# Two Q units between the fold blocks, residual copies two tiles ahead, sums by quarter: one change in four parts to a fused attention and mixer block

## The chip, the cores and the metric

The kernel runs on one core of one Trainium2 chip. The metric is the device time of one execution in microseconds (us). A profiled execution stands beside the timed runs; its span is the time from the first to the last instruction of the core.

Engines are named as in the profile: PE is the matrix engine (PEld its weight loads), DVE the vector engine, ACT the scalar engine, POOL the general engine, SP the engine that issues most of the DMAs. SPq is SP's queue.

## The reference

`x` is 2048 x 1024 (S x D) in bf16. The block is two residual parts:

```
h  = x + o(LN(x)) @ wo          # linear attention, 32 heads of 32
     q, k, v = split(LN(x) @ wqkv);  phi(t) = where(t > 0, t + 1, exp(t)) + 1e-6
     kv = phi(k)^T v per head;  z = sum over rows of phi(k)
     o  = (phi(q) kv) / (phi(q) . z + 1e-6)
h2 = h + mixer(LN(LN(h)))       # LN of LN: the mixer normalizes its own input again
     u  = gelu(hn^T @ w1 + b1)          # w1: 2048 x 3584, over the rows of x
     y  = (u @ w2 + b2)^T               # w2: 3584 x 2048
```

## The kernel before, in words

**Products in blocks of seven.** All large products are done as two-by-two block products with seven multiplications instead of eight: sums of blocks of the one operand (`asum`, `asums`, `x_sums`) and of the other (`combine`, `inner_moving`, `w_sums`) are made on DVE, and PE adds seven products into PSUM tiles. In the mixer, two of the seven (later more) are again split by seven (`Inner`, `Inner2`). A product's method `mm` (L355) walks over the `nk` blocks of the contracted dimension, one 128 x 128 x 512 matmul each.

**Order.** Most instructions are kept in program order on their engine by `pin` or by the wrappers `hv` (DVE), `ht` (PE), `hs` (ACT), `hd` (SP DMAs), so the order in which the Python code issues them is the order on each engine. A tile of a pool waits for the last reader of the buffer that it gets.

**Stage 1, to about 163 us in the profile: K, V, Q.** Rows of x are normalized and transposed (`ln_finish`). From row pair 2 on, K and V of two row tiles are a step each (`KRun`, `VRun`), and Q of a quarter of the rows comes in steps `QRun` with pairs 5 and 7 and after them. `run_step` (L1239) interleaves a step with the rest of the previous one. Q of the first quarter is done in eight plain units of eight matmuls: `q_unit` (L1419) and, later, `q_held` (L1645). Each unit's phi is one Exp and one Relu on ACT and two operations on DVE. `q_fill` takes the next of the eight. Three are issued around the first V step, one each after step `p7` of K and V of pair 6 (`fill_at`, L1463), one in the last `run_step`. Two are left for the fold stretch.

**Fold stretch, 163 to 177 us.** `kv` and `wo` are multiplied into one weight per head: `fold(n)` (L1629), n = 0 to 3, is 16 matmuls of 32 x 32 x 512 into four PSUM tiles; ACT and DVE copy these to `wf` (fp16): block 1 on DVE, for the second half of the columns (n = 1, 3) block 3 too, the others on ACT. Folds 0 and 2 give columns 0 to 511, folds 1 and 3 the rest. `den_mm` makes the denominators of a quarter of rows, `den_inv` their reciprocals, `den_spread` sends them through DRAM to all partitions, and `scale_q` (DVE, 128 x 2048) multiplies phi(q) by them. `q_held(units[0])` uses one of two PSUM banks of the pool of the denominators (`den_tile`), as do two tiles of `fold(2, 2)`. All others come from `acc_tile` (L83), a ring of six banks in two pools of four and two.

**Output projection, 169 to 229 us: loop over 16 row tiles** (L1810), in the order of quarters 2, 3, 1, 0 (`SPREAD`, `order`). Tile i is two halves of eight matmuls (`out_mm`), evacuated by `out_evac`. For the first nine tiles (`SEEDED` = 9) a DMA from POOL adds x to the evacuated tile (L1715); means and squares come from ACT's accumulators or DVE. From tile 9 on the residual is put into the PSUM bank ahead of the matmuls: `seed(i)` (L1673) is two ACT copies of the loaded row tile (`load_xr`), and DVE takes the statistics straight from PSUM. `h_var` and `store_h` issue the tile's store on SP; `h_scale` is Ln and Exp on ACT; `normalize_h` (DVE) writes the even row tiles into `hE`, the odd into `hO`; as soon as a pair is there, `combine_h` (L1758) makes its four sums, each 128 x 512: T3 = O.hi - E.hi, E.hi = E.hi - E.lo, T2 = O.hi - E.hi, T4 = O.lo - T2. W1 is loaded in column groups of 512 in four parts (`load_w1`, L146): group 0 in the fold stretch, group 1 at tiles 5, 7, 9 and 11 (`w1_at`). `first_sums` makes the first weight sums of the mixer in between.

In this loop a seed of tile i+1 stands first in iteration i from tile 10 on; seeds of 9 and 10 come in iterations 7 and 8, behind `out_evac(i)`.

**Mixer, 229 us to the end.** PSUM pools psy, psx, psw, psz of two banks each are opened (L1861). `sums5` makes the four inner sums of E.hi (128 x 1024 each), then `run_first` (L759) does product 1 (E.lo), product 2 (O.lo), then inner product 5 mixed with product 6 (T2), then 7 (T3) and 3; product 4 (T4) comes with the next pair of column groups. Mixer 1 contracts over eight row blocks, in the order 0 to 7: block k holds row tiles 2k (in `hE`) and 2k+1 (in `hO`). The last quarter of the projection, quarter 0, is blocks 0 and 1; quarter 1 is blocks 2 and 3.

Of the kernel before, what the change touches and what calls it, by code (L numbers as in the profile page):

```python
# [24 lines left out]
SEEDED = 9  # L25
# [8 lines left out]
def kernel(  # L34
# [144 lines left out]
    def combine(e, o, t2, t3, t4, v=nc.vector):  # L179
        lo, hi = slice(0, CW), slice(CW, 2 * CW)  # L180
        sub = ALU.subtract
        v.tensor_tensor(t3, o[:, hi], e[:, hi], sub)
        v.tensor_tensor(e[:, hi], e[:, hi], e[:, lo], sub)
        v.tensor_tensor(t2, o[:, hi], e[:, hi], sub)
        if t4 is not None:
            v.tensor_tensor(t4, o[:, lo], t2, sub)

# [144 lines left out]
    class Product7:  # L332
        def __init__(self, p, w, nk, mov):
# [21 lines left out]
        def mm(self, m, ps, start, ks=None, cols=slice(0, CW)):  # L355
            lhs, mv = self.lhs[m], self.mov[m]
            for k in range(self.nk) if ks is None else ks:
                pe.matmul(
                    ps[:, cols],
                    lhsT=lhs[:, k, :],  # L360
                    rhs=mv(k)[:, cols],
                    start=(start and k == 0),
                    stop=(k == self.nk - 1),
                    skip_group_check=True,
                )
# [73 lines left out]
    class Mixer1(Product7):  # L439
        def __init__(self, p):  # L440
# [428 lines left out]
    with ExitStack() as actx:  # L869
# [33 lines left out]
        with ExitStack() as a1:  # L903
# [559 lines left out]
            fill_at = {("K", 6, 0), ("V", 6, 0)}  # L1463
# [161 lines left out]
        with ExitStack() as a3:  # L1625
# [125 lines left out]
            def normalize_h(i, combined=True):  # L1751
# [3 lines left out]
                if combined and i ^ 1 in normal:  # L1755
                    combine_h(i)

            def combine_h(i):  # L1758
                q = order[i] // 2
                combine(hE[:, q, :], hO[:, q, :], hT2[:, q, :], hT3[:, q, :], hT4[:, q, :], hv)  # L1760
# [18 lines left out]
            fold(2, 2)  # L1779
            scale_q(2, 1)  # L1780
            load_w1(0, 1, pin, 4)
            q_held(*units[1])
            fold(1)
            load_w1(0, 2, pin, 4)
            xctx.close()
# [23 lines left out]
            w1_at = {5: (1, 0), 7: (1, 1), 9: (1, 2), 11: (1, 3)}  # L1809
            for i in range(1, NS):  # L1810
                if i > SEEDED:
                    seed(i + 1)
# [8 lines left out]
                if i == NS - 1:  # L1821
                    h_scale(i - 1)
                    normalize_h(i - 2, False)
# [3 lines left out]
                if i - 3 in BY_ACT:  # L1827
                    normalize_h(i - 3)
                if i > 1:
# [3 lines left out]
                if SEEDED - 2 <= i < SEEDED:  # L1833
                    seed(i + 2)
# [15 lines left out]
                if SEEDED + 2 <= i < NS - 1:  # L1850
                    normalize_h(i - 2)
            h_scale(NS - 1)
            normalize_h(NS - 1, False)
            combine_h(NS - 3)
            combine_h(NS - 1)
# [4 lines left out]
    NT = 2  # L1860
# [229 lines left out]
```

## Time and profile before

| what | value |
|---|---|
| timed runs | 553.98, 555.28, 552.6 us; median 553.98 |
| profiled execution, its own time | 553.12 us |
| its span | 551.3 us |
| granted PE clock | 1.000 |
| fold stretch, first held Q unit to the den matmuls of tile 1 | 162.75 to 177.39 us |
| output projection, den matmuls of tile 3 to the first mixer product | 184.95 to 229.30 us |

A row of the timeline is: start, length in us, engine, line, operation, output<-input, partitions x elements and type, count; in brackets the idle time of the engine before it and what ended it. Matmul lengths include the drain of the pipeline, so the distance between starts says how fast PE goes. A row of the waits list is: the engine and its tile, the releaser, total us, times, longest. A row of the windows view is: stretch, length, busy time of PE, PEld, DVE, ACT, POOL (with counts), granted clock, share of the DMA engines, GB/s.

### The profile page before, as it was taken

To read this page: it belongs to the slowest core of one execution; us is meant where nothing else is said; L and a number is where in the kernel's file an instruction comes from. 1 tells how busy PE (TensorE), PEld (TensorE's weight loads), DVE (VectorE), ACT (ScalarE), POOL (GpSimd) and SP (SyncE) were. 2 spreads that over 40 slices of the span, in tenths; PEclk is the share of its full clock that TensorE was granted. 3 is DMA by queue.
4 is the path that set the end of the run, shared out by engine and by line. 5 is a ranking of instruction groups with operands and counts; after the bars stand their busy time and mean duration, and the time that the engine had idled before them with its cause. 6 is when DMAs were issued, how large, how long until landed. Compare 5 with 4: busy or idle time off the path is not lost.

```text
span 551.3 us, 10262 instructions
## 1 busy us (share of the span) xinstructions
PE 542.7 (98%) x3978; PEld 331.8 (60%) x3978; DVE 462.6 (84%) x904; ACT 292.3 (53%) x630; POOL 42.3 (8%) x54
## 2 busy tenths in 40 slices
PE   8999999999999998999999999999999999999997
PEld 3444446646763443456666767667455667877865
DVE  7798898866776698989989789897989899979877
ACT  5747777777687778545546465464320312413321
POOL 1000000000002350000000000000002102103111
PEclk9999999999999999999999999999999999999999
DMA  9933531200537999203140440413497659399344
GB/s 300 311 78 76 78 82 35 40 0 3 153 110 212 210 278 355 98 2 112 42 153 9 145 137 19 153 33 102 125 315 210 187 123 243 80 289 236 68 136 76
DMA packets 84513, 74.61 MB, mean 135 GB/s; under 512 B 16098, under 2 KB 77040, under 8 KB 84464
## 3 DMA queue, kind: packets, MB, share of 16 engines
q1 hardware_dynamic: 77344, 67.46, 41.6%
q0 software_dynamic: 6688, 6.04, 7.7%
q8 instruction: 31, 0.51, 0.4%
q10 hardware_dynamic: 432, 0.44, 0.2%
q14 instruction: 18, 0.15, 0.1%
HBM read 59.12 MB, written 11.67 MB: 128 GB/s over the span
## 4 chain that ended last, share of the span: by engine, by line
PE 89%; issue 2%; DMA 2%; ACT 2%; DVE 2%; POOL 1%; SPq 0%; DVEq 0%; POOLq 0%; ACTq 0%
PE psI L245 28%; PE psC L245 17%; PE psB L245 8%; PE acc_t L245 4%; PE psC L1071 4%; PE psB L1071 4%; PE psA L1071 4%; PE psA L245 3%; PE acc_t L987 3%; PE psE L1071 2%; PE psA L1205 2%; PE psC L1205 2%; PE psB L1205 2%; PE acc_t L1422 2%; POOL h_bf L1715 1%
## 5 line engine op out<-in xcount | busy, mean ns | idle before, releaser
L245 PEld LDWEIGHTS <-is 128*128 128x128 f16 x820 | 80.1, 98 | 31.5 <-DVE hi L245 0.4
L245 PEld LDWEIGHTS <-wq 128*128 128x128 bf16 (+1 forms) x610 | 59.6, 98 | 38.6 <-issue 1.0
L245 PEld LDWEIGHTS <-sa 128*128 128x128 f16 x571 | 55.8, 98 | 20.7
L245 PE MATMUL acc_t<-wo_sb,pqT 128*128 128x512 f16 x256 | 56.3, 379 | 3.0 <-ACT acc_t L245 2.2
L513 POOL DMA_DIRECT2D out_dram<-wq x28 | 24.4, 949 | 310.9 <-DMA wq<-in_B_w_dram 191.0
L245 PEld LDWEIGHTS <-pqT 128*128 128x128 bf16 x256 | 24.8, 98 | 33.9 <-issue 3.6
L245 PE MATMUL psC<-gs,wq 128*128 128x512 f16 x168 | 40.8, 379 | 0.0
L1071 PEld LDWEIGHTS <-xs 128*128 128x128 f16 x208 | 20.0, 98 | 22.2
L245 PE MATMUL psC<-hT,sa 128*128 128x512 f16 x112 | 31.2, 379 | 0.0
L1715 POOL DMA_DIRECT2D h_bf<-in_A_x_dram x18 | 15.9, 995 | 186.3 <-PE acc_t L245 171.1
L245 PE MATMUL psI<-hi,is 128*128 128x256 f16 x200 | 30.0, 273 | 0.0
L245 PE MATMUL psB<-hT,sa 128*128 128x512 f16 x112 | 29.7, 379 | 0.0
L245 DVE TENSOR_TENSOR t<-psI,t 128x256 f32<-128x256 f32 (+1 forms) x45 | 20.8, 475 | 9.4 <-PE psI L245 7.9
L245 PE MATMUL psC<-hT,wq 128*128 128x512 f16 x112 | 28.4, 379 | 0.0
L245 PE MATMUL psI<-gi,is 128*128 128x256 f16 x210 | 27.8, 273 | 0.0
L1071 PE MATMUL psA<-wkv,xnT 128*128 128x512 bf16 x104 | 26.7, 379 | 0.0
L1071 PEld LDWEIGHTS <-xnT 128*128 128x128 bf16 x156 | 15.3, 98 | 17.8 <-issue 0.2
L198 DVE TENSOR_SCALAR e_sb<-e_sb 128x512 bf16<-128x512 bf16 x64 | 18.2, 284 | 7.6 <-ACT e_sb L193 7.4
L245 ACT COPY psI<-psI 128x256 f32<-128x256 f32 x50 | 18.0, 360 | 11.7 <-PE psI L245 9.8
L245 DVE TENSOR_TENSOR sa<-wq 128x2048 f16<-128x2048 bf16 (+1 forms) x17 | 20.0, 1178 | 2.8 <-DMA wq<-in_B_w_dram 2.8
L987 PE MATMUL acc_t<-wkv,xnT 128*128 128x512 bf16 x96 | 21.7, 379 | 0.1
L956 DVE BATCH_NORM_STATS2 st<-x_sb 128x6 f32<-128x512 bf16 x32 | 20.6, 682 | 0.9 <-DMA x_sb<-in_A_x_dram 0.9
(266 smaller groups left out, 1145.4 us busy)
## 6 DMA issues: line engine op xcount, KB each, us to landing
wq<-in_B_w_dram SPq DMA_DIRECT2D x10, 1024.0 KB, 7.1
wq<-in_B_w_dram SPq DMA_DIRECT2D x20, 448.0 KB, 6.6
gs<-parked SPq DMA_DIRECT2D x9, 896.0 KB, 4.8
shared_sb<-rd_dram SPq DMA_DIRECT2D x32, 128.0 KB, 3.9
wq<-in_B_w_dram SPq DMA_DIRECT2D x8, 512.0 KB, 7.8
out_dram<-h_bf SPq DMA_DIRECT2D x16, 256.0 KB, 5.9
x_sb<-in_A_x_dram SPq DMA_DIRECT2D x14, 256.0 KB, 4.1
w2o<-in_B_w_dram SPq DMA_DIRECT2D x4, 896.0 KB, 10.2
```

The source lines that it names most:

```text
L198: pin(nc.vector.tensor_scalar(e_sb[:], e_sb[:], 1.0, PHI_EPS, ALU.min, ALU.add))
L245: return (lambda *a, **kw: pin(op(*a, **kw))) if self.always or getattr(Held, self.key) else op
L513: nc.gpsimd.dma_start(to, ot[:, a:b], accum_op=ALU.add)
L956: return nc.vector.bn_stats(st[:, c, :], x_sb[:, c * CW:(c + 1) * CW])
L987: mm = nc.tensor.matmul(pp[:, 0:CW], lhsT=xnT[:, kt, i * P:(i + 1) * P], rhs=wkv[:, kt, c * CW:(c + 1) * CW], start=(kt == 0), stop=(kt == ...
L1071: pin(nc.tensor.matmul(ps[:], lhsT=lhs[:, k, :], rhs=rhs[:, k, :], start=(start and k == 0), stop=(k == hk2 - 1), skip_group_check=True,))
L1205: pin(nc.tensor.matmul(out[:, j], lhsT=rhs[:, k, 2 * self.half + j, :], rhs=lhs[:, k], start=(start and j == 0 and k == 0), stop=(k == hk2 ...
L1422: nc.tensor.matmul(qp[:, 0:SW], lhsT=wq_sb[:, kt, j * P:(j + 1) * P], rhs=xnT[:, kt, u * SW:(u + 1) * SW], start=(kt == 0), stop=(kt == ND ...
L1715: nc.gpsimd.dma_start(h_bfs[i][:, cols], x[rows(i), cols], accum_op=ALU.add)
```

## The change

Four things are changed.

1. `fill_at` is empty: the K and V steps of pair 6 have no Q unit. Four units are left for the fold stretch: one before fold 0 (den bank), one after fold 0 (ring bank), one after fold 2 and one after fold 1 (den banks). `fold(2)` takes all its tiles from the ring.
2. `seed(i + 2)` for i = 7 to 13 stands ahead of `out_evac(i)`. Group 1 of W1 is loaded at tiles 9 to 12.
3. `combine` is gone. `sums_h(u, which)` makes the sums of a whole quarter (four row tiles) in operations of 128 x 2 x 512: of quarter 2 at tiles 7 and 8, of quarter 3 at tiles 11 and 12, of quarters 1 and 0 without T4 after the last statistics, with the normalization of tile 15 between them. T4 of those two quarters is one operation of 128 x 4 x 512 after `sums5`.
4. `Mixer1.first = NSP // 4` = 2: its products walk the row blocks in the order 2, 3, 4, 5, 6, 7, 0, 1. The four PSUM pools of the mixer are opened in the opposite order.

```diff
@@ -176,15 +176,6 @@
             for ks in spans:
                 load_w2(p, second, ks=ks)
 
-    def combine(e, o, t2, t3, t4, v=nc.vector):
-        lo, hi = slice(0, CW), slice(CW, 2 * CW)
-        sub = ALU.subtract
-        v.tensor_tensor(t3, o[:, hi], e[:, hi], sub)
-        v.tensor_tensor(e[:, hi], e[:, hi], e[:, lo], sub)
-        v.tensor_tensor(t2, o[:, hi], e[:, hi], sub)
-        if t4 is not None:
-            v.tensor_tensor(t4, o[:, lo], t2, sub)
-
     def phi_parts(dst, src, n, pool, view=lambda t: t, lean=False):
         e_sb = pool.tile([P, n], BF16, tag="phi_e", name="e_sb")
         r_sb = None if lean else pool.tile([P, n], BF16, tag="phi_r", name="r_sb")
@@ -330,6 +321,8 @@
             self.sink(0, 1, self.b)
 
     class Product7:
+        first = 0
+
         def __init__(self, p, w, nk, mov):
             self.p, self.nk, self.mov = p, nk, mov
             (self.a11, self.a21), (self.a12, self.a22) = [[v[:, :, h * P:(h + 1) * P] for h in range(2)] for v in w]
@@ -355,10 +348,11 @@
         def mm(self, m, ps, start, ks=None, cols=slice(0, CW)):
             lhs, mv = self.lhs[m], self.mov[m]
             for k in range(self.nk) if ks is None else ks:
+                at = (k + self.first) % self.nk
                 pe.matmul(
                     ps[:, cols],
-                    lhsT=lhs[:, k, :],
-                    rhs=mv(k)[:, cols],
+                    lhsT=lhs[:, at, :],
+                    rhs=mv(at)[:, cols],
                     start=(start and k == 0),
                     stop=(k == self.nk - 1),
                     skip_group_check=True,
@@ -437,6 +431,8 @@
                 self.after(self.done, late)
 
     class Mixer1(Product7):
+        first = NSP // 4
+
         def __init__(self, p):
             c = (p % 2) * 2 * P
             w = w1_tiles[p // 2][:, :, c:c + 2 * P].rearrange("p (k two) f -> p k two f", two=2)
@@ -1460,7 +1456,7 @@
             q_sums = {2: slice(0, 1), 3: slice(1, 2), 4: slice(2, 3), 5: slice(3, 4)}
             late_parts, late_home = sums_home(2)
             moved_at = {("K", 7, 0): ((3, 0), (3, 1)), ("V", 7, 0): ((4, 0), (4, 1))}
-            fill_at = {("K", 6, 0), ("V", 6, 0)}
+            fill_at = set()
             late_sums = {("K", 6): ((2, slice(0, 2)),), ("K", 7): ((2, slice(2, 4)), (3, slice(0, 1))), ("V", 7): ((3, slice(1, 4)),)}
             for q in range(2, NVP):
                 runs = [KRun(q), VRun(q)]
@@ -1748,16 +1744,25 @@
                 hs.activation(lnv[:], mv_all[:, i, 1:2], ACT.Ln, bias=eps2[:], scale=(1.0 + LN_EPS) * share_of)
                 hs.activation(sc_all[:, i:i + 1], lnv[:], ACT.Exp, scale=-0.5)
 
-            def normalize_h(i, combined=True):
+            def normalize_h(i):
                 dst = hE if i % 2 == 0 else hO
                 hv.tensor_scalar(dst[:, order[i] // 2, :], h_bfs.pop(i)[:], mv_all[:, i, 0:1], sc_all[:, i:i + 1], ALU.subtract, ALU.mult)
                 normal.add(i)
-                if combined and i ^ 1 in normal:
-                    combine_h(i)
-
-            def combine_h(i):
-                q = order[i] // 2
-                combine(hE[:, q, :], hO[:, q, :], hT2[:, q, :], hT3[:, q, :], hT4[:, q, :], hv)
+
+            lo, hi = slice(0, CW), slice(CW, D)
+
+            def sums_h(u, which=("t3", "t1", "t2", "t4")):
+                assert normal.issuperset(range(NSC * SPREAD.index(u), NSC * SPREAD.index(u) + NSC))
+                ks = slice(NSC // 2 * u, NSC // 2 * (u + 1))
+                e, o = hE[:, ks], hO[:, ks]
+                for t in which:
+                    out, p, q = {
+                        "t3": (hT3[:, ks], o[:, :, hi], e[:, :, hi]),
+                        "t1": (e[:, :, hi], e[:, :, hi], e[:, :, lo]),
+                        "t2": (hT2[:, ks], o[:, :, hi], e[:, :, hi]),
+                        "t4": (hT4[:, ks], o[:, :, lo], hT2[:, ks]),
+                    }[t]
+                    hv.tensor_tensor(out, p, q, ALU.subtract)
 
             def first_sums():
                 cur = Quad([Mixer1(0), Mixer1(1)])
@@ -1776,12 +1781,14 @@
             scale_q(2, 0)
             den_spread(3, 1)
             load_w1(0, 0, pin, 4)
-            fold(2, 2)
+            q_held(*units[1])
+            fold(2)
             scale_q(2, 1)
             load_w1(0, 1, pin, 4)
-            q_held(*units[1])
+            q_held(*units[2], den_tile())
             fold(1)
             load_w1(0, 2, pin, 4)
+            q_held(*units[3], den_tile())
             xctx.close()
             a3w = a3.enter_context(tc.tile_pool(name="a3w", bufs=8))
             squares = a3.enter_context(tc.tile_pool(name="sqpool", bufs=1)).tile([P, D], BF16, name="squares")
@@ -1806,10 +1813,9 @@
             scale_at = {1: (3, 0), 2: (3, 1), 4: (1, 0), 5: (1, 1), 8: (0, 0), 9: (0, 1)}
             den_at, sums_at = {1: 1, 3: 0}, (1, 2, 3, 5, 6)
             spread_at = {1: ((1, 0), (1, 1)), 4: ((0, 0),), 5: ((0, 1),)}
-            w1_at = {5: (1, 0), 7: (1, 1), 9: (1, 2), 11: (1, 3)}
+            w1_at = {9: (1, 0), 10: (1, 1), 11: (1, 2), 12: (1, 3)}
+            sums_h_at = {7: ((2, ("t3", "t1")),), 8: ((2, ("t2", "t4")),), 11: ((3, ("t3", "t1")),), 12: ((3, ("t2", "t4")),)}
             for i in range(1, NS):
-                if i > SEEDED:
-                    seed(i + 1)
                 if i > 1:
                     out_mm(i)
                 if i in den_at:
@@ -1820,18 +1826,18 @@
                     load_xr(i + 5)
                 if i == NS - 1:
                     h_scale(i - 1)
-                    normalize_h(i - 2, False)
+                    normalize_h(i - 2)
                     normalize_h(i - 1)
                 if 1 < i <= SEEDED:
                     h_mean(i - 1)
                 if i - 3 in BY_ACT:
                     normalize_h(i - 3)
+                if SEEDED - 2 <= i < NS - 2:
+                    seed(i + 2)
                 if i > 1:
                     out_evac(i)
                 if i - 3 in BY_DVE:
                     h_scale(i - 3)
-                if SEEDED - 2 <= i < SEEDED:
-                    seed(i + 2)
                 if i - 2 in BY_ACT:
                     h_var(i - 2)
                     h_scale(i - 2)
@@ -1849,19 +1855,21 @@
                     h_var(i - 2)
                 if SEEDED + 2 <= i < NS - 1:
                     normalize_h(i - 2)
+                for at in sums_h_at.get(i, ()):
+                    sums_h(*at)
             h_scale(NS - 1)
-            normalize_h(NS - 1, False)
-            combine_h(NS - 3)
-            combine_h(NS - 1)
+            sums_h(1, ("t3", "t1", "t2"))
+            normalize_h(NS - 1)
+            sums_h(0, ("t3", "t1", "t2"))
             less_acc()
 
     earlyctx.close()
     actx_psum.close()
     NT = 2
+    psz = ctx.enter_context(tc.tile_pool(name="psz", bufs=NT, space=PSUM, reuse_waits="tile"))
+    psw = ctx.enter_context(tc.tile_pool(name="psw", bufs=NT, space=PSUM, reuse_waits="tile"))
+    psx = ctx.enter_context(tc.tile_pool(name="psx", bufs=NT, space=PSUM, reuse_waits="tile"))
     psy = ctx.enter_context(tc.tile_pool(name="psy", bufs=NT, space=PSUM, reuse_waits="tile"))
-    psx = ctx.enter_context(tc.tile_pool(name="psx", bufs=NT, space=PSUM, reuse_waits="tile"))
-    psw = ctx.enter_context(tc.tile_pool(name="psw", bufs=NT, space=PSUM, reuse_waits="tile"))
-    psz = ctx.enter_context(tc.tile_pool(name="psz", bufs=NT, space=PSUM, reuse_waits="tile"))
     gpool = ctx.enter_context(tc.tile_pool(name="gpool", bufs=1))
     gE = gpool.tile([P, NFP, D], FP16, name="gE")
     gO = gpool.tile([P, NFP, D], FP16, name="gO")
@@ -1891,6 +1899,8 @@
 
     Held.on = Held.scalar = True
     sums5()
+    late = slice(0, NSP // 2)
+    dve.tensor_tensor(hT4[:, late], hO[:, late, 0:CW], hT2[:, late], ALU.subtract)
     cur.mov5 = mov5
     pend, nxt = cur.run_first(quad1(1), sums1, sums2)
     for u in range(1, NQ1):
```

## The prediction

> **What bounds the kernel now.** I read the page's engine shares first, then who waited for whom on PE in stretches of the span, then the timeline of the two stretches where PE waits.
>
> ```profile
> span 551.3 us, 10262 instructions
> PE 542.7 (98%) x3978; PEld 331.8 (60%) x3978; DVE 462.6 (84%) x904; ACT 292.3 (53%) x630; POOL 42.3 (8%) x54
> PE acc_t L245 <- DVE wo_sb L245: 0.7, 2, 0.5
> PE den_ps L245 <- ACT r_sb L195: 0.6, 1, 0.6
> PE acc_t L245 <- ACT acc_t L245: 2.2, 1, 2.2
> ```
>
> PE is the bound, so only its waits can be won. From 30 us to the end the waits list shows just these three groups: two in the fold stretch (160 to 180 us) and one in the output projection. "Busy" hides part of a wait, so I count matmuls too. A 512-column matmul takes 0.216 us in a full pipe (24.35 us for 112, below), eight take 1.73, an output tile of sixteen 3.46.
>
> ```profile
> 162.75 1.89 PE L245 MATMUL den_ps<-xnT,wq_sb 128*128 128x512 bf16 x8
> 164.57 0.60 PE L245 MATMUL acc_t<-wo_sb,shared_sb 32*32 32x512 bf16 x17
> 166.29 1.89 PE L245 MATMUL acc_t<-xnT,wq_sb 128*128 128x512 bf16 x8
> 168.11 0.43 PE L245 MATMUL acc_t<-wo_sb,shared_sb 32*32 32x512 bf16 x16
> 169.06 2.17 PE L245 MATMUL acc_t<-wo_sb,pqT 128*128 128x512 f16 x8 [0.52 <-DVE wo_sb L245]
> 177.39 0.62 PE L245 MATMUL den_ps<-pqT,zz 128*32 128x512 bf16 x8
> 185.50 24.35 PE L245 MATMUL acc_t<-wo_sb,pqT 128*128 128x512 f16 x112
> 212.03 17.43 PE L245 MATMUL acc_t<-wo_sb,pqT 128*128 128x512 f16 x80 [2.19 <-ACT acc_t L245]
> ```
>
> **Fold stretch.** From the first held Q unit (162.75) to the den matmuls (177.39) are 14.64 us. The work is two Q units and four half tiles (6 x 1.73 = 10.4) and four folds at 0.36 (168.11 to 168.47): 11.8. So 2.8 us are waits, of which the list shows 1.3. **Output projection.** Between 185.50 and 229.30 there is one hole, 2.19 us ahead of tile 11. Both holes together are 5.0 us, nearly all that this change can win.
>
> **The change part by part.**
>
> *Two Q units leave V/K pair 6 for the fold blocks.* Each takes 8 x 0.216 = 1.73 us of PE, so the V/K stretch gets 3.46 us shorter and the fold stretch gets the same work. The question is whether the pair still runs without waits when the cover goes.
>
> ```profile
> 58.00:71.00 13.00, 13.00 (x182) 6.40 (x165) 11.23 (x25) 9.20 (x21) 0.00 (x0) 1.00 0.49 79
> 111.00:119.00 8.00, 8.00 (x38) 3.62 (x37) 5.24 (x14) 6.49 (x12) 0.00 (x0) 1.00 0.00 0
> ```
>
> The columns are stretch, length, PE, PEld, DVE, ACT. Earlier pairs run without fill units at 13.00 of 13.00 with DVE at 11.23 and ACT at 9.20. Pair 6 has 5.24 of DVE and 6.49 of ACT in 8 us, and of those a unit's Exp and Relu (about 1.0) and its two DVE operations (0.7) go with it: 5.5 of ACT in 6.3. I take 0; if the cover was needed the price is up to both units, +3.46.
>
> In the fold stretch I replay each engine's order after the change from these rows; T is the start of the first held unit.
>
> ```profile
> 164.00:170.00 6.00, 4.80 (x63) 1.67 (x61) 5.76 (x11) 5.88 (x14) 0.00 (x0) 1.00 0.34 98
> 164.68 0.60 ACT L193 ACTIVATE e_sb<-den_ps 128x512 bf16<-128x512 f32 x1
> 165.65 2.06 ACT L245 CAST wo_sb<-acc_t 128x512 f16<-128x512 f32 x4
> 166.59 0.68 DVE L245 CAST wo_sb<-acc_t 128x512 f16<-128x512 f32 x1
> 167.19 1.22 DVE L245 TENSOR_TENSOR pqT<-pqT,shared_sb 128x2048 bf16<-128x2048 bf16 x1
> ```
>
> ACT is full there (5.88 of 6 us). Its pitch is 0.48 us (Exp and Relu from 164.68 to 165.65), it takes the first Exp at T+1.93 (164.68), and it has eight Exp/Relu and ten copies to do. PE: unit 0 to T+1.73, fold 0 to 2.2, unit 1 to 3.95 (in a ring bank that is free). Fold 2 no longer takes den banks; it takes banks of fold 0, the last of which DVE frees at T+4.52 (167.27): 0.6 us of wait, done 4.85. Unit 2 runs in a den bank to 6.6. Fold 1's bank 3 is that of fold 2's block 1, which DVE copies behind the scaling and unit 1's phi, until T+7.0: 0.4 us of wait, done 7.4. Unit 3 runs to 9.13. The half tile of output then finds the scaling done (T+8.2), goes to 10.9, fold 3 to 11.25, the next half to 13.0, just when ACT has freed the bank of the first (three copies from 11.4: 12.95). Two more end at 16.5. Without the change this point is T+14.64, and T now lies 3.46 earlier: 14.64 + 3.46 - 16.5 = **1.6 us won**. At best the waits go wholly (2.8). At worst ACT, full already and given 2 us more, keeps a pitch nearer the 0.60 that one operation lasts: 18 x 0.12 = 2.2 later, and nothing is won (0).
>
> *Residual copies two tiles ahead.* This is the chain in front of the hole.
>
> ```profile
> 206.05 1.15 ACT L245 ACTIVATE squares<-h_bf,mv_all 128x1024 bf16<-128x1024 bf16 x1 [0.92 <-DMA h_bf<-in_A_x_dram]
> 207.76 1.05 ACT L245 CAST h_bf<-acc_t 128x512 bf16<-128x512 f32 x2
> 209.69 1.15 ACT L245 ACTIVATE squares<-h_bf,mv_all 128x1024 bf16<-128x1024 bf16 x1 [0.88 <-DVE hst L245]
> 211.40 1.09 ACT L245 CAST acc_t<-shared_sb 128x512 f32<-128x512 bf16 x2
> 200.88 0.35 SPq L245 DMA_DIRECT2D shared_sb<-in_A_x_dram  x1
> 208.36 1.29 DVE L245 BATCH_NORM_STATS2 hst<-acc_t 128x6 f32<-128x512 f32 x2
> 209.90 1.22 DVE L245 TENSOR_TENSOR pqT<-pqT,shared_sb 128x2048 bf16<-128x2048 bf16 x1
> ```
>
> Tile 11's copy (211.40) stands behind the evacuation of tile 9 (207.76) and the squares of tile 7 (209.69), both of which came after a wait. Moved in front of that evacuation it can start at 207.76, and its first half is done by 208.4, ahead of the 209.8 at which PE gets there. The wait that is added: the copy of tile i+2 needs its load and the banks of tile i-1; behind it on ACT stand the evacuation of tile i and squares, and behind those the statistics (DVE), the store and the next load (SP), for tiles 7 and 8 the adding DMA (POOL). Tile 11's load was issued at 200.88; with the longest latency below it lands at 210.1, with the median at 208.7, so ACT may stand 0.9 us. Then tile 12: tile 9's evacuation ends at 210.9, its statistics near 212.0; squares and Ln/Exp take 1.71 (209.69 to 211.40) to 212.6, so the copy's first half is there at 213.2, and PE asks at 213.3 (209.85 + 3.46). That is the brim; if squares wait for the statistics, as at 209.69, it is 0.5 late. The scaling of quarter 0 (209.90) slips behind the statistics, to 213.2, and is just in time. From there ACT needs 2.7 us a tile (1.09 + 1.05 + 0.56) against 3.46 and runs free. So the hole shrinks from 2.19 to 0.2: **2.0 won**; between 1.0 (loads at their longest) and 2.2.
>
> *W1 loads of pair 1 moved from tiles 5, 7, 9, 11 to 9 to 12.* Four issues, each ahead of that tile's residual load in SP's order.
>
> ```profile
> wq<-in_B_w_dram SPq DMA_DIRECT2D x7, 512.0 KB, 7.9
> shared_sb<-in_A_x_dram SPq DMA_DIRECT2D x7, 256.0 KB, 7.8
> DMA to landing us min/median/max: 3.2/6.1/9.2
> 213.20 0.34 SPq L245 DMA_DIRECT2D shared_sb<-in_A_x_dram  x1
> 200.00:205.00 5.00, 5.00 (x25) 2.29 (x24) 4.82 (x14) 4.94 (x14) 3.37 (x4) 1.00 1.13 301
> 215.00:220.00 5.00, 5.00 (x24) 2.25 (x23) 4.79 (x13) 4.14 (x12) 0.00 (x0) 1.00 1.06 400
> 243.38 0.42 DVE L245 TENSOR_TENSOR is<-wq 128x512 f16<-128x512 bf16 x1
> ```
>
> The DMA share stands above 1 (last column but one) around tiles 6 to 12. A megabyte less before tile 9 is about 3.5 us of transfer at 301 GB/s, in favour of the loads of tiles 10 to 13 and of the additions that squares wait for; I count it as cover for the 0.9 us above, not as gain. From tile 9 on the queue carries 2 MB of W1, five stores and two loads, 3.9 MB in 13.8 us or 280 GB/s, where 400 were moved. The last W1 part goes out during tile 12, before 221, and has until 243. Price 0 while the loads of tiles 14 and 15 arrive in time (rival D). The Trainium skill says, in "DMA: Bandwidth & Descriptors", section "Queues, rings and completion order", that each SDMA engine takes descriptors of one row in ring order and takes turns between rows by packet. By that rule GpSimd's additions gain little from the move, while a residual load behind W1 waits for all of it; as an estimate, 1.7 us for 512 KB at 301 GB/s, and about 1 us off the sum. The trace of before can't show it, since W1 parts stood between the loads all along.
>
> *Sums by quarter, last rows last.* A 1024-element difference stands at a pitch of 0.72 (235.61 to 236.33), and two of 512 last 0.42 each (the row at 243.38), 0.84 without their gaps; so DVE is relieved a little during tiles 4 to 14. But six sums now follow the last statistics.
>
> ```profile
> 229.30 3.62 PE L245 MATMUL psA<-hE,wq 128*128 128x512 f16 x16
> 230.85 0.21 DVE L245 BATCH_NORM_AGGREGATE mv_all<-hst 128x2 f32<-128x12 f32 x1
> 235.61 0.69 DVE L245 TENSOR_TENSOR hi<-hE 128x1024 f16<-128x1024 f16 x1
> 236.33 0.69 DVE L245 TENSOR_TENSOR hE<-hE 128x1024 f16<-128x1024 f16 x1
> 240.70 0.42 DVE L245 TENSOR_TENSOR e<-psI,es 128x256 f32<-128x256 f32 x1 [0.82 <-PE psI L245]
> 237.81 0.61 PE L245 MATMUL psI<-hi,is 128*128 128x256 f16 x4
> ```
>
> With E = 229.30: three sums from E+1.76 end at 3.92, tile 15 is normalized by 4.5, three more sums to 6.54, and the third of the inner sums ends at 8.7. PE wants tile 15's row, now the last of eight, at E+3.45+1.5 = 4.95: hidden. It wants the third inner sum at E+8.42 and before had it at 8.51; now 8.75: **0.25 lost** (0 to 0.8, if DVE enters E late). The T4 half (2048 elements, nearest row the scaling at 1.22) falls where DVE stood idle (0.82 ahead of 240.70) and delays nothing that PE wants before 242.4.
>
> The turned PSUM pools put the first mixer tiles on den banks, free since tile 3; psA started without a wait before: 0.
>
> **Sum**: -1.6 - 2.0 + 0.25 + 0 = -3.35. The profiled execution took 553.12 us (span 551.3): 549.8. The median of the three runs, 553.98, lies 0.86 higher and would give 550.6. I take 550.2.
>
> **Rivals.** **A: ACT binds the fold stretch.** For it: ACT at 5.88 of 6. Against: the waits that show there are for banks, and the held units fill just these. Fold gain 0: -1.75, 551.8. **B: the holes close wholly.** -5.0, 548.5. For it: DVE and DMA are relieved ahead of both; against: the bank waits in my replay. **C: the units were cover in pair 6.** Full price +3.46: 553.7, no change. Against: pairs 3 and 4 at 13.00 of 13.00. **D, the other side: a residual load arrives late and ACT stands.** The place is the copy of tile 15: its load is issued at 213.20, now right behind a W1 part, and PE wants the copy at 223.7 (209.85 + 4 x 3.46), less 0.6 for its first half. Up to 9.9 us of latency it costs nothing; each us beyond is one for PE, with evacuations and stores queued behind. The gain is gone at 13.2 and slower by over 0.5% begins at 16; at 18 it is 557.9. For it: the bunched W1; against: 9.2 is the longest here, and the queue had room (280 against 400). **That the change doesn't do what it says** (the ring hands a copy a bank of a tile not yet evacuated, so that it runs one tile ahead as before) keeps the 2.19: 552.2; I count it with A.
>
> **How the numbers follow.** Forecast (gain 2.6 to 4.3) 0.54, A 0.16, B 0.11, C 0.09, D 0.10. A measurement of this kernel can tell about 0.5%, 2.8 us, from no change. Faster by more: B and nine tenths of the forecast, 0.60; slower: D, 0.10; between: 0.30. The range goes from B (548.4) to between A and C (553.0).
>
> **What would show it.** The first fill-less step of pair 6 at 109.5 with psA right behind psC; 17.0 us or less from the first held unit to the den matmuls; no wait of PE for acc_t in the output projection above 0.5; inner sums' matmul at E+8.75. Wrong: a new PE wait near 110 to 120 (C), ACT waiting for shared_sb loads (D), or the fold stretch near 18 us (A).

## The result, and the profile after

| | before | after |
|---|---|---|
| median of the timed runs | 554.17 us (552.6 to 555.28, 6 runs) | 550.7 us (549.93 to 551.81, 6 runs) |
| profiled execution, its own time | 553.12 us | 551.11 us |
| its span | 551.3 us | 549.2 us |

The ratio is 0.9941, with a 95% interval of 0.992 to 0.9961. In a later comparison it was 0.9946 (0.9927 to 0.9966). The page of the kernel after, its span and engine shares:

```profile
span 549.2 us, 10234 instructions
PE 541.3 (99%) x3962; PEld 331.7 (60%) x3978; DVE 459.1 (84%) x887; ACT 292.0 (53%) x630; POOL 42.0 (8%) x54
```

The waits list of the kernel after, PE from 30 to 300 us (total, times, longest):

```profile
PE psI L236 <- DVE hi L236: 0.5, 1, 0.5
PE psA L236 <- ACT psB L236: 0.4, 1, 0.4
PE acc_t L236 <- DVE wo_sb L236: 0.2, 1, 0.2
```

The wait of 2.2 for a residual copy is gone, the three waits of the fold stretch have become one, and two new ones stand where the mixer begins. No wait appears in the V/K stretch. I now go through the stages by the starts of PE's rows. First pair 6, before and then after; each row is the first group of one K or V step:

```profile
103.46 1.03 PE L1071 MATMUL psA<-wkv,xnT 128*128 128x512 bf16 x4
...
111.25 1.03 PE L1071 MATMUL psA<-wkv,xnT 128*128 128x512 bf16 x4
...
119.02 1.03 PE L1071 MATMUL psA<-wkv,xnT 128*128 128x512 bf16 x4
```

```profile
103.89 1.03 PE L1067 MATMUL psA<-wkv,xnT 128*128 128x512 bf16 x3
...
109.95 1.03 PE L1067 MATMUL psA<-wkv,xnT 128*128 128x512 bf16 x4
...
115.99 1.03 PE L1067 MATMUL psA<-wkv,xnT 128*128 128x512 bf16 x4
```

The two steps take 15.56 us before and 12.10 after: 3.46 less, the whole length of two units. (The start, 0.43 later, comes from a wait in the first 30 us that neither version touches.) Next, PE's timeline of the kernel after through the fold stretch:

```profile
159.72 1.89 PE L236 MATMUL den_ps<-xnT,wq_sb 128*128 128x512 bf16 x8
...
164.29 0.43 PE L236 MATMUL acc_t<-wo_sb,shared_sb 32*32 32x512 bf16 x14 [0.17 <-DVE wo_sb L236]
...
166.49 0.71 PE L236 MATMUL acc_t<-wo_sb,shared_sb 32*32 32x512 bf16 x16
167.13 1.90 PE L236 MATMUL den_ps<-xnT,wq_sb 128*128 128x512 bf16 x7
...
176.34 0.62 PE L236 MATMUL den_ps<-pqT,zz 128*32 128x512 bf16 x8
```

From the first held unit to the den matmuls are 16.62 us (14.64 before): 1.98 longer with 3.46 more work in it, so 1.48 won. Fold 2 still waits (its last 14 matmuls start at 164.29), and fold 1 lasts 0.71 instead of 0.43. Then the projection and the first mixer products, PE's timeline of the kernel after:

```profile
184.44 41.65 PE L236 MATMUL acc_t<-wo_sb,pqT 128*128 128x512 f16 x192
225.93 3.71 PE L236 MATMUL psA<-hE,wq 128*128 128x512 f16 x16
230.03 3.61 PE L236 MATMUL psA<-hO,wq 128*128 128x512 f16 x16 [0.39 <-ACT psB L236]
...
235.68 0.61 PE L236 MATMUL psI<-hi,is 128*128 128x256 f16 x4 [0.52 <-DVE hi L236]
```

E is again the start of the first mixer product, 225.93 here. All 192 matmuls of tiles 4 to 15 are one row without a break. From the den matmuls of tile 1 to the first mixer product are 49.59 us (51.91 before): 2.32 won. But from there to the second inner product are 9.75 us instead of 8.51: product 2 starts at E+4.10 (E+3.45 is full pace), and the inner product then waits for `hi`. This handoff loses 1.24. In all: -1.48 - 2.32 + 1.24 + 0.43 = -2.13, which is 549.2 less 551.3, up to the rounding.

Why the handoff is late, in DVE's timeline of the kernel after, the first statistics taken from PSUM (tile 9) and the last aggregate (tile 15):

```profile
209.43 1.29 DVE L236 BATCH_NORM_STATS2 hst<-acc_t 128x6 f32<-128x512 f32 x2 [0.97 <-ACT h_bf L236]
...
228.72 0.21 DVE L236 BATCH_NORM_AGGREGATE mv_all<-hst 128x2 f32<-128x12 f32 x1
```

Before, these two were at 208.36 and 230.85, and the aggregate was at E+1.55: that is about the least, since tile 15 has to be evacuated behind E first (DVE waited 0.31 us for it). The chain had 22.49 us between them, with 0.7 of idle. After, it is 3.2 us shorter (19.29, idle 0.5), mostly because of the sums by quarter: four operations of 0.69 us stand in it where twelve of 0.42 stood. But PE's way from the first of these statistics to E shrank by 4.4 (20.94 to 16.50), and so the aggregate comes at E+2.79, 1.24 too late. A second profile of the same kernel (after_timed below) bears this out: the chain is again 19.29 us long, but starts 16.91 us ahead of E, 0.41 earlier; the aggregate is at E+2.38 and the handoff takes 9.34, both 0.41 less. Part of the lateness is the later start, in ACT's timeline of the kernel after:

```profile
206.09 1.15 ACT L236 ACTIVATE squares<-h_bf,mv_all 128x1024 bf16<-128x1024 bf16 x1 [1.77 <-DMA h_bf<-in_A_x_dram]
...
207.79 1.09 ACT L236 CAST acc_t<-shared_sb 128x512 f32<-128x512 bf16 x2
208.82 1.06 ACT L236 CAST h_bf<-acc_t 128x512 bf16<-128x512 f32 x2
...
229.40 1.06 ACT L236 COPY psB<-psA 128x512 f32<-128x512 f32 x2
```

The evacuation of tile 9, for which those statistics wait, starts at 208.82 (before 207.76), 2.1 us later when counted from the den matmuls of tile 1: one half is the copy of tile 11 ahead of it, the other the addition for which the squares wait (1.77 us here, 1.14 in the second profile). The last row is the two copies that product 2 waits for; they stand behind Ln and Exp of tile 15, which wait for the aggregate. And the windows view of the kernel after shows that DVE had no time to catch up (stretch, length, busy time of PE, PEld and DVE):

```profile
221.00:226.00 5.00, 5.00 (x25) 2.29 (x24) 4.90 (x11) 3.35 (x9) 0.00 (x0) 1.00 0.41 154
```

**Theory**: the hole ahead of tile 11 was also the time in which DVE and ACT caught up with PE. Closing it leaves DVE's chain from tile 9 to the inner sums as the bound of the handoff. **Rivals**: the sums by quarter themselves make DVE late at the end, or the turned block order does; and the moved W1 loads are what closed the hole.

### The profile page after: what moved, and what is told of

It reads as the page before. It is cut to its first block, busy times and chain, and to the rows that moved or that the text cites. A ratio compares the mean times of both kernels' runs of the same rounds, so it can differ in the third digit from the quotient of the medians.

```text
span 549.2 us, 10234 instructions
## 1 busy us (share of the span) xinstructions
PE 541.3 (99%) x3962; PEld 331.7 (60%) x3978; DVE 459.1 (84%) x887; ACT 292.0 (53%) x630; POOL 42.0 (8%) x54
## 2 busy tenths in 40 slices
DMA packets 84512, 74.60 MB, mean 136 GB/s; under 512 B 16098, under 2 KB 77040, under 8 KB 84464
## 4 chain that ended last, share of the span: by engine, by line
PE 86%; DVE 4%; DMA 3%; issue 3%; ACT 2%; POOL 1%; SPq 1%; DVEq 0%; POOLq 0%; ACTq 0%
PE psI L236 29%; PE psC L236 18%; PE psB L236 8%; PE psC L1067 4%; PE psB L1067 4%; PE psA L1067 4%; PE acc_t L983 3%; PE psA L236 2%; PE psE L1067 2%; PE psA L1201 2%; PE psC L1201 2%; PE psB L1201 2%; PE acc_t L236 2%; DVE hst L236 2%; DMA wkv<-in_A_wqkv_dram 1%
## 5 line engine op out<-in xcount | busy, mean ns | idle before, releaser
L1067 PE MATMUL psA<-wkv,xnT 128*128 128x512 bf16 x96 | 25.6, 379 | 0.4
L236 ACT COPY psI<-psI 128x256 f32<-128x256 f32 x50 | 18.0, 360 | 12.1 <-PE psI L236 10.2
```

What stands on the lines that cost most here:

```text
L236: return (lambda *a, **kw: pin(op(*a, **kw))) if self.always or getattr(Held, self.key) else op
L1067: pin(nc.tensor.matmul(ps[:], lhsT=lhs[:, k, :], rhs=rhs[:, k, :], start=(start and k == 0), stop=(k == hk2 - 1), skip_group_check=True,))
```

## The experiments

Each row has the stages as read above: **fold** from the first held unit to the den matmuls of tile 1, **projection** from there to the first mixer product, **handoff** from there to the second inner product, **both** the sum of these two, **rest** from there to the end of the span.

| kernel | fold | projection | handoff | both | rest | span |
|---|---|---|---|---|---|---|
| before | 14.64 | 51.91 | 8.51 | 60.42 | 313.5 | 551.3 |
| after | 16.62 | 49.59 | 9.75 | 59.34 | 313.5 | 549.2 |
| units_only | 16.62 | 51.85 | 8.51 | 60.36 | 313.5 | 550.6 |
| sums_only | 14.64 | 51.81 | 8.52 | 60.33 | 313.5 | 551.6 |
| old_sums | 16.62 | 49.62 | 12.37 | 61.99 | 314.0 | 552.2 |
| seed_behind | 16.62 | 50.35 | 8.60 | 58.95 | 313.5 | 548.4 |
| deferred | 16.62 | 49.55 | 8.42 | 57.97 | 314.6 | 548.9 |
| def_mix | 16.62 | 49.82 | 8.60 | 58.42 | 314.3 | 549.0 |
| w1_early | 16.62 | 49.56 | 9.65 | 59.21 | 313.5 | 549.3 |
| first0 | 16.62 | 49.92 | 9.65 | 59.57 | 314.1 | 549.8 |
| after_timed | 16.62 | 49.55 | 9.34 | 58.89 | 313.6 | 549.7 |
| behind_timed | 16.61 | 50.11 | 8.59 | 58.70 | 313.5 | 548.9 |
| deferred_timed | 16.62 | 49.56 | 8.42 | 57.98 | 314.4 | 548.7 |
| def_fold | 16.38 | 49.93 | 8.42 | 58.35 | 313.9 | 548.0 |

**units_only**: the kernel before, with the two Q units moved and nothing else.

```diff
-            fill_at = {("K", 6, 0), ("V", 6, 0)}
+            fill_at = set()
...
-            fold(2, 2)
+            q_held(*units[1])
+            fold(2)
...
-            q_held(*units[1])
+            q_held(*units[2], den_tile())
             fold(1)
             load_w1(0, 2, pin, 4)
+            q_held(*units[3], den_tile())
```

> The kernel before with the moved Q units alone. Stages: fold stretch (first held Q unit to the den matmuls of tile 1; 14.64 us before, 16.62 after), projection (from there to the first mixer product; 51.9 and 49.6), handoff (from there to the second inner product; 8.51 and 9.75). Theory, the closed hole ahead of tile 11 was also the time in which ACT and DVE caught up, and the handoff pays for it: fold stretch 16.5 to 16.8 with the V/K pair 3.46 shorter, so 1.4 to 1.6 us won; the hole of about 2 us stays, projection 51.5 to 52.1; handoff 8.4 to 8.7. Rival, the units brought ACT into arrears that reach the end: handoff 9.3 or more already here.

PE's timeline:

```profile
211.29 17.43 PE L245 MATMUL acc_t<-wo_sb,pqT 128*128 128x512 f16 x80 [2.13 <-ACT acc_t L245]
228.56 3.62 PE L245 MATMUL psA<-hE,wq 128*128 128x512 f16 x16
...
237.07 0.61 PE L245 MATMUL psI<-hi,is 128*128 128x256 f16 x4
```

One run took 552.39 us (before, on the same chip: 552.92). The fold stretch is the one of the whole change, the hole keeps its 2.13, and the handoff its 8.51. Part 1 wins its 1.5 us alone and costs nothing later.

**sums_only**: the kernel before, with the sums by quarter and the turned block order (parts 3 and 4).

```diff
-                    normalize_h(i - 2, False)
+                    normalize_h(i - 2)
...
-            normalize_h(NS - 1, False)
-            combine_h(NS - 3)
-            combine_h(NS - 1)
+            sums_h(1, ("t3", "t1", "t2"))
+            normalize_h(NS - 1)
+            sums_h(0, ("t3", "t1", "t2"))
...
     class Mixer1(Product7):
+        first = NSP // 4
```

> The kernel before with the sums by quarter and the order of the row blocks alone. Theory (the hole was catch-up time): hole about 2.2 us, projection 51.9, and as the hole is still there DVE is not late, handoff 8.3 to 8.8. Rival, the placing of the sums at tiles 11 and 12 and behind the last statistics makes DVE late: handoff 9.4 or more.

It took 553.41 us beside 552.92: nothing won, the hole stays at 2.10 and the handoff at 8.52. So neither the quarter sums nor the turned order makes the handoff late by itself; with the hole closed, old_sums and first0 below test them. With the hole open, their relief of DVE is worth nothing either.

**old_sums**: the kernel after, with the sums pair by pair as before (part 3 undone).

```diff
-            sums_h_at = {7: ((2, ("t3", "t1")),), 8: ((2, ("t2", "t4")),), 11: ((3, ("t3", "t1")),), 12: ((3, ("t2", "t4")),)}
...
-            sums_h(1, ("t3", "t1", "t2"))
-            normalize_h(NS - 1)
-            sums_h(0, ("t3", "t1", "t2"))
+            normalize_h(NS - 1, False)
+            combine_h(NS - 3)
+            combine_h(NS - 1)
```

> The kernel after with the sums made pair by pair as before, so the moved units and the residual copies two tiles ahead remain. Theory: fold stretch 16.6, projection 49.6 (no hole), and DVE late all the same, handoff 9.5 to 10.5. Rival, the quarter sums are what makes DVE late: handoff 8.4 to 8.9.

The waits list of PE, and the last aggregate in DVE's timeline:

```profile
PE psA L245 <- DVE hE L245: 2.4, 2, 1.9
```

```profile
231.29 0.21 DVE L245 BATCH_NORM_AGGREGATE mv_all<-hst 128x2 f32<-128x12 f32 x1
```

It took 554.0 us: no faster than before. The direction is the theory's, the size larger than I expected (12.37, not 9.5 to 10.5): DVE's chain from tile 9 takes 22.18 us, nearly as before, and with the hole closed it ends at E+5.44, so that the first product already waits. Everything that parts 1 and 2 won is lost in the handoff. Part 3, worth nothing with part 4 alone, is what makes part 2 pay.

**seed_behind**: the kernel after, with the copy of tile i+2 behind the evacuation of tile i.

```diff
-                if SEEDED - 2 <= i < NS - 2:
-                    seed(i + 2)
                 if i > 1:
                     out_evac(i)
+                if SEEDED - 2 <= i < NS - 2:
+                    seed(i + 2)
```

> The kernel after with the copy of tile i+2 behind the evacuation of tile i instead of ahead of it. Theory, lateness is set by when DVE's run without a break starts: the evacuations of tiles 9 and 10 and their statistics come 1 us earlier, there is still no hole (projection 49.5 to 49.8), and the handoff is 8.7 to 9.1. Rival, the sum of DVE's work from tile 9 on decides: handoff 9.5 to 9.8 as in the kernel after. Second rival, the place in front was needed: PE waits 0.3 us or more ahead of tile 11 or 12.

PE's timeline, then DVE's:

```profile
208.82 17.67 PE L236 MATMUL acc_t<-wo_sb,pqT 128*128 128x512 f16 x80 [0.39 <-ACT acc_t L236]
226.32 3.62 PE L236 MATMUL psA<-hE,wq 128*128 128x512 f16 x16
...
234.92 0.60 PE L236 MATMUL psI<-hi,is 128*128 128x256 f16 x4
```

```profile
207.82 1.29 DVE L236 BATCH_NORM_STATS2 hst<-acc_t 128x6 f32<-128x512 f32 x2
...
227.88 0.21 DVE L236 BATCH_NORM_AGGREGATE mv_all<-hst 128x2 f32<-128x12 f32 x1
```

Tile 9's statistics start 18.5 us ahead of E instead of 16.5, the last aggregate is at E+1.56, the least that there is, and the handoff takes 8.60. So DVE is no longer late. But 0.76 of that is PE's own delay, most of it ahead of tile 11, whose copy is late again by a part of the old hole. Projection and handoff together take 58.95 us, and 58.70 in behind_timed, against 59.34 and 58.89 in the two profiles of the changed kernel: most of the loss has only moved from the one side to the other. Both accounts, the catch-up and the late copy, are true at once.

**deferred**: less of DVE's work ahead of the inner sums.

```diff
-            sums_h_at = {7: ((2, ("t3", "t1")),), 8: ((2, ("t2", "t4")),), 11: ((3, ("t3", "t1")),), 12: ((3, ("t2", "t4")),)}
+            sums_h_at = {7: ((2, ("t3", "t1")),), 8: ((2, ("t2", "t4")),), 12: ((3, ("t1", "t2")),)}
...
-            sums_h(1, ("t3", "t1", "t2"))
+            sums_h(1, ("t1", "t2"))
...
-            sums_h(0, ("t3", "t1", "t2"))
+            sums_h(0, ("t1", "t2"))
...
     sums5()
+    for ks in (early, late):
+        dve.tensor_tensor(hT3[:, ks], hT2[:, ks], hE[:, ks, 0:CW], ALU.subtract)
...
             before_inner(slice(2, 4))
+            after_inner()
```

(`early` is row blocks 0 to 3, `late` 6 and 7; `after_inner` makes T4 of both.)

> The changed kernel with less of DVE's work ahead of the inner sums: T3 of quarters 3, 1 and 0 is made after the inner sums as T2 - E.lo (the same values up to rounding), T4 of quarter 3 with the T4 of the other two, behind the sums of product 1's operand. Theory (DVE enters the handoff late, because it never caught up): two operations of 0.72 less ahead of the last statistics and two less behind them; the last aggregate starts near E+1.4 (was E+2.79), the third inner sum ends near E+7 (was E+9.5), handoff 8.4 to 8.6 (was 9.75), projection unchanged at 49.6, so 1.2 less in all, near 549.9. Rival: the lateness only moves on, and PE waits for DVE between 236 and 262 us for the 2.9 us of sums that now stand there; then the waits list has a new PE wait for t, e, is or hT and the time stays within 0.5 of the changed kernel's.

PE's timeline, then DVE's:

```profile
225.86 3.62 PE L236 MATMUL psA<-hE,wq 128*128 128x512 f16 x16
229.32 3.62 PE L236 MATMUL psA<-hO,wq 128*128 128x512 f16 x16
...
234.28 0.60 PE L236 MATMUL psI<-hi,is 128*128 128x256 f16 x4
...
248.05 0.60 PE L236 MATMUL psI<-hi,is 128*128 128x256 f16 x4 [0.19 <-ACT psI L236]
...
402.46 3.19 PE L236 MATMUL psB<-gT,gi 128*128 128x512 f16 x14 [0.26 <-DVE gi L236]
```

```profile
227.48 0.21 DVE L236 BATCH_NORM_AGGREGATE mv_all<-hst 128x2 f32<-128x12 f32 x1
```

The last aggregate is at E+1.62, product 2 starts at full pace (E+3.46), and the handoff takes 8.42, the 8.42 of matmuls without any wait, with the projection unchanged. Only the place of DVE's sums was changed, so the lost 1.2 us were DVE's. But of the 1.33 won only 0.3 reach the end (span 548.9, 550.65 us): 0.35 go at 248, where PE waits for a copy of ACT that stands behind an activation held up by DVE's sums, much as the rival had it, and 0.75 before and at 402, at the first weights of mixer 2. There the DMA rows read (tile, KB, median us to landing), of deferred and of the kernel after:

```profile
wq<-in_B_w_dram SPq DMA_DIRECT2D x4, 448.0 KB, 7.6
```

```profile
wq<-in_B_w_dram SPq DMA_DIRECT2D x4, 448.0 KB, 6.7
```

These loads go out when PE frees the buffer, so they move with it; only their landing differs.

**def_mix**: as deferred, with the copies of tiles 12 to 15 behind the evacuation.

```diff
-                if SEEDED - 2 <= i < NS - 2:
+                if SEEDED - 2 <= i <= SEEDED:
                     seed(i + 2)
                 if i > 1:
                     out_evac(i)
+                if SEEDED < i < NS - 2:
+                    seed(i + 2)
```

> As deferred, and the residual copies of tiles 12 to 15 stand behind the evacuation of the tile in hand, those of 9 to 11 ahead of it as in the changed kernel. If only tile 11's copy was late before the change, the projection stays at 49.6 to 49.8 and the statistics come earlier; handoff 8.4 to 8.5, time as deferred or 0.3 less. If the later copies need to be ahead too, the projection loses up to 0.75, as with all copies behind, and the time is near 550.5.

It took 550.79 us. Projection and handoff take 58.42 us, 0.45 more than in deferred: nothing won. The later copies are wanted ahead too, for 0.27 of it; the other 0.18 is in the handoff (8.60), and why it was not 8.4 to 8.5 was not traced.

**w1_early**: the kernel after, with the W1 parts back at tiles 5, 7, 9 and 11.

```diff
-            w1_at = {9: (1, 0), 10: (1, 1), 11: (1, 2), 12: (1, 3)}
+            w1_at = {5: (1, 0), 7: (1, 1), 9: (1, 2), 11: (1, 3)}
```

> The changed kernel with the W1 parts back at tiles 5, 7, 9 and 11. If SP's W1 parts hold back only what stands behind them in SP's own queue, the additions that ACT's squares wait for land as before (median 6.9, the wait of squares near 206 us stays 1.8) and only the residual loads get slower again (6.4 to 7 or 8); projection 49.6 to 49.9. Rival, all queues share one bandwidth: the additions land later (7.5 or more), squares wait 0.5 to 1 us longer, tile 11's copy is late and a hole of 0.5 to 1.5 comes back ahead of tile 11.

The DMA rows from 184 to 226 us, of w1_early and of the kernel after:

```profile
shared_sb<-in_A_x_dram SPq DMA_DIRECT2D x7, 256.0 KB, 7.8
h_bf<-in_A_x_dram POOLq DMA_DIRECT2D x12, 128.0 KB, 6.6
```

```profile
shared_sb<-in_A_x_dram SPq DMA_DIRECT2D x7, 256.0 KB, 6.4
h_bf<-in_A_x_dram POOLq DMA_DIRECT2D x12, 128.0 KB, 6.9
```

It took 551.14 us, and projection and handoff 59.21: the move of W1 is worth nothing, and the hole stays closed without it. The residual loads, in SP's queue like W1, get slower, and ACT now waits for the one of tile 12:

```profile
211.58 1.11 ACT L236 CAST acc_t<-shared_sb 128x512 f32<-128x512 bf16 x2 [0.59 <-DMA shared_sb<-in_A_x_dram]
```

The additions, in POOL's queue, do not get slower; the squares of tile 6 wait 0.85 for theirs here, and 1.77 and 1.14 in the two profiles of the changed kernel. What the chain wins at the one place it loses at the other. The other profiles say the same of the queues: in the four kernels with W1 at tiles 5 to 11 the residual loads land at medians of 7.8 to 8.2 us, in the ten with W1 at tiles 9 to 12 at 6.0 to 6.5, but for two (7.2 in behind_timed, 7.7 in def_fold); the additions land at 6.6 to 7.1 and 6.5 to 7.5. The rival, one shared bandwidth that makes the hole return, falls. The Trainium skill's rule ("DMA: Bandwidth & Descriptors", section "Queues, rings and completion order": one row's descriptors in ring order, turns between rows by packet) agrees with these rows: POOL's additions gained nothing from the move, and a load behind W1 came late.

**first0**: the kernel after, with the old block order (part 4 undone).

```diff
     class Mixer1(Product7):
-        first = NSP // 4
+        first = 0
```

> The changed kernel with mixer 1's products walking the row blocks from 0 again. Product 2 then wants the row of tile 15 as its second of eight: PE stands from about E+4.3 to E+5.4, where DVE has normalized it. Since the third inner sum comes at E+9.5 anyhow, part of that is hidden: handoff 10.2 to 10.4 (was 9.75), projection unchanged. If the two waits add, 10.9; if DVE's sums alone set it, 9.75.

PE's timeline:

```profile
226.90 3.40 PE L236 MATMUL psA<-hE,wq 128*128 128x512 f16 x15 [0.44 <-DVE hE L236]
...
230.81 3.40 PE L236 MATMUL psA<-hO,wq 128*128 128x512 f16 x15 [0.30 <-DVE hO L236]
```

PE waits 0.9 for rows of the last tiles, yet projection and handoff take 59.57 us, 0.2 and 0.7 more than in the two profiles of the changed kernel (59.34 and 58.89), and 9.65 is within what those two took for the handoff. As long as DVE's sums are late, they set the second inner product, and the turned order mainly changes at which product PE waits. My 10.2 to 10.4 was wrong; two profiles of one kernel that differ by 0.45 don't settle what is left. The total, 551.66 us, has 0.55 from the rest (below).

**Timed together**, five rounds on one chip, before at 553.34 us (14 runs): after_timed is the changed kernel, behind_timed is seed_behind, deferred_timed is deferred, and def_fold is deferred with another order of the held units.

> The changed kernel once more, on the chip of the three others: 550.7, ratio 0.994 to the kernel before.

> All residual copies behind the evacuation in hand: in one look it lost 0.75 in the projection and won 1.15 in the handoff, 0.4 net and the tail unchanged at 313.5 from the second inner product to the end: 550.3.

> The deferred sums: in one look the handoff was 1.33 shorter than in the changed kernel, but the tail from the second inner product to the end was 314.6 instead of 313.5, most of it where the first W2 group landed later (median 7.6 us against 6.7). If that landing varies from run to run, the median is near 549.6 and the spread wide; if W2 comes at that time whatever the kernel, the time is near 550.4, a third of a us better than the changed kernel.

```diff
             q_held(*units[1])
+            q_held(*units[2], den_tile())
             fold(2)
...
-            q_held(*units[2], den_tile())
+            q_held(*units[3], den_tile())
             fold(1)
             load_w1(0, 2, pin, 4)
-            q_held(*units[3], den_tile())
```

> As deferred, and the third held unit ahead of fold 2, the fourth ahead of fold 1. If the 0.84 us that are left in front of and within folds 2 and 1 are bank waits, the stretch falls from 16.62 to 15.8 to 16.0; if ACT, which is busy without a break from 159 to 168.6, sets it, it stays at 16.6. The gain would then go the way of the deferred one, as far as W2 lets it.

| kernel | median, us | runs | ratio to before, 95% interval |
|---|---|---|---|
| after_timed | 550.89 | 8 | 0.9946 (0.9927 to 0.9966) |
| behind_timed | 550.24 | 6 | 0.9932 (0.9906 to 0.9957) |
| deferred_timed | 550.43 | 7 | 0.9934 (0.991 to 0.9958) |
| def_fold | 549.74 | 6 | 0.9926 (0.9903 to 0.9949) |

Each variant is below the changed kernel by its median, def_fold by 1.15 us; the intervals overlap, so the order among them is not settled by the times alone. PE's timeline of def_fold shows where its fold stretch went:

```profile
167.33 0.54 PE L236 MATMUL acc_t<-wo_sb,shared_sb 32*32 32x512 bf16 x16
...
169.63 0.70 PE L236 MATMUL acc_t<-wo_sb,shared_sb 32*32 32x512 bf16 x16
170.50 5.34 PE L236 MATMUL acc_t<-wo_sb,pqT 128*128 128x512 f16 x24 [0.17 <-DVE wo_sb L236]
...
211.89 13.97 PE L236 MATMUL acc_t<-wo_sb,pqT 128*128 128x512 f16 x64 [0.21 <-ACT acc_t L236]
```

Fold 2's wait is gone and fold 1 is shorter, but fold 3 (169.63 to 170.50) takes 0.87 where it took 0.37. Of 0.84 us only 0.24 were won; behind fold 3 PE waits for DVE's copy of a fold block, so these copies are probably the limit by now, which was not tried. And the projection is 0.38 longer than in deferred: PE waits for the copy of tile 12 (211.89), behind squares that waited 0.88 and 0.18 us for additions, which landed at a median of 7.5 us here and at 7.0 and 6.8 in deferred and deferred_timed. Fold, projection and handoff together take 74.73 us against 74.59 and 74.60, so in its profile the new order won nothing on the way. Its shorter span comes from the rest (313.9 against 314.6 and 314.4), where the first weights of mixer 2 landed earlier (last section), and from the first 30 us.

## Why the prediction was right, and which step failed

The forecast, 550.2 us, was 0.5 below the median and the time is well within the range. That the total came so near is in part luck: the stages that the change touches moved by 2.56 us in the profile above and by 3.01 in the second profile, not by 3.35, and the medians differ by 3.47 in the first comparison and by 2.45 in the later one (553.34 to 550.89). Step by step:

- **Two Q units into the fold stretch: right.** 1.6 forecast, 1.48 measured. The replay holds mark by mark: with T = 159.72, unit 3 starts at T+7.41 (forecast 7.4), the den matmuls at T+16.62 (16.5), and fold 2 and fold 1 have the two short bank waits. Pair 6 lost exactly the units' 3.46: rival C is wrong. Rival A is wrong for the change as made; def_fold suggests that it stands just behind.
- **Copies two tiles ahead: right**, 2.0 forecast, 2.32 measured, a little over the bound of 2.2. The copy of tile 11 moved from 211.40 to 207.79 and the whole hole closed. PE never waited for a late residual load, so rival D did not come. Nor did the "about 1 us off the sum" that I worked out from the rule of the Trainium skill ("DMA: Bandwidth & Descriptors", section "Queues, rings and completion order"). The 0.9 us of cover that I gave to the W1 move was not needed: without the move the projection is the same, and only 0.59 of ACT's time goes to a late load.
- **The handoff: the mis-sized term.** 0.25 forecast with a bound of 0.8; measured 1.24, and 0.83 in the second profile of the same kernel. The step that failed is "three sums from E+1.76". I took DVE's entry from the trace of before and named its lateness only as a bound. DVE enters at E+2.79 (E+2.38 in the second profile), because DVE's chain from tile 9's statistics had only 0.7 us of slack in 22.49 before. My other steps changed both sides, and I did not carry them to the end: the closed hole and the later start took 4.4 us from PE's way, and 3.2 went from DVE's, most of it by the sums by quarter, which I called "a little" relief (2.9 by old_sums). The difference is the 1.24, and the sign that I gave, the inner sums' matmul at E+8.75, came at E+9.75. Longer sums (old_sums) and fewer (deferred) move the handoff to 12.37 and to 8.42, with the projection the same. From the last aggregate to the third inner sum it went as replayed: in seed_behind, where the aggregate stands at E+1.56, the handoff takes 8.60.
- **T4 half, turned pools: right**, the rest is 313.5 us in both kernels and product 1 starts without a wait.
- **The sum**: -3.35 forecast; -2.56 by the stages that the change touches, and -2.13 with the 0.43 by which the first 30 us were longer in that execution.
- **Rival B** (both holes close wholly) was half right: the projection's did, the fold stretch's did not, and part of the gain became the new wait.

The parts are not additive: sums_only won nothing by its stages and units_only 1.5 (0.5 of it in its one run; in its profile the first 30 us were 0.8 longer than in that of before), while the change without part 3 (old_sums) is as slow as the kernel before.

## What to carry to other kernels

A hole in the bound engine can also be the time in which its helpers catch up, as DVE did here. Before a hole is closed, take the helper's chain from the hole to the next handover, set its length beside the bound engine's way over the same stretch, and replay both with every edit in them. An instruction that is moved ahead in an engine's order delays all that stands behind it by its own length, and the price shows on another engine, many tiles later; relief that is worth nothing alone may be what pays for it.

## What the runs showed beside that

**The first weights of mixer 2 stand at the brim.** With a median landing of 6.7 to 7.0 us they cost nothing (after, units_only, sums_only, seed_behind: rest 313.5). The three kernels with the deferred sums lose 0.35 at 248 us; beyond that, 7.2 and 7.2 us cost about 0.5 (deferred_timed, def_mix), 7.6 cost 0.75 (deferred), 6.9 nothing (def_fold), and in first0 7.3 cost 0.55. The same kernel landed at 7.6 and 7.2 in two executions. What sets the landing was not tried. The rest of old_sums is 0.5 longer at a landing of 6.9; where that goes I did not trace.

**The first 30 us vary.** The K step of pair 6 starts between 103.46 and 104.80 us in fourteen profiles, while the code ahead of it is the same in all, and at 31 us PE's rows already stand as far apart (31.03 to 32.37). That is 1.3 us of the spread of the times, as large as the term that I had wrong.
